# The output stage of an FFT filter with soft experts: combine weights on strips of 32 PE rows in float32r

## The chip, the cores and the metric

The kernel runs on one core of a Trainium2 chip. The time is what the device takes for one execution, in microseconds (us); work that the host does before and after is outside it. Before the change it is 431.18 us, the median of three runs (430.67, 431.18 and 431.85). Engines have these names: PE is TensorE (PEld its weight loads), DVE is VectorE, ACT is ScalarE, POOL is GpSimd, SP is the engine that here issues the DMA transfers.

## The reference

The input x is 8 batches of 2496 rows with 256 features. First it is filtered along the rows by a Fourier transform; then a layer of soft experts (8 experts with 4 slots each, so 32 slots) is applied to all 19968 filtered rows together:

```
X = rfft(x, axis=1);  y = irfft(X * F, n=2496)      # F: 1249 x 256, complex
logits = y @ phi                                    # 19968 x 32
d = softmax of logits over all rows                 # dispatch weights, one column per slot
slot_input = d.T @ y                                # 32 x 256
slot_out[e] = relu(slot_input[e] @ w1[e]) @ w2[e]   # hidden size 1024
c = softmax of logits over the 32 slots of a row    # combine weights
out = c @ slot_out                                  # 19968 x 256, float32
```

The last line is the output stage: for each row a product of its 32 combine weights with the 32 x 256 matrix slot_out. It writes 20.45 MB.

## The kernel before, in words

The transform of a batch is factored: 2496 = 39 x 64, with the row number written as 64 s1 + s2. The host lays out x so that a step i (0 to 21) holds up to three values of s2 (j = 0, 1, 2; PK = 3), each with its 39 values of s1, on 117 partitions (KR = 117). A table (RUNS) says which s2 belongs to a step and a j: in steps 0 to 15 j counts 0, 16 and 32 upwards, in steps 16 to 19 it counts 48, 52 and 56, and steps 20 and 21 hold the last four, s2 = 60 to 63 (step 20 three of them, step 21 one). The stages ahead of the output work through the batches in a pipeline, form the logits in the layout of these steps, and gather the slot inputs over groups of batches (GROUPS). For each group a tile with the exponentials of the logits is left (lgs; the first two groups are parked in DRAM and read back) with 117 partitions and, for every step, batch and slot, one element; r_all holds the reciprocals of the row sums. Then the expert products run (lines 786 to 820), in strips of 32 PE columns, with weights read from DRAM, and slot_out stands in PSUM, four times over on 128 partitions.

The output stage begins at line 821. It uses float32r, in which a matmul streams faster but keeps fewer bits, and makes up for the bits with high and low parts: so_h is slot_out rounded to float32r, and so holds so_h on partitions 0 to 63 and the remainder on 64 to 127. For the combine weights the same is done in `combine` (line 837), called for up to four steps at once, six times a batch:

- GpSimd multiplies the exponentials by the reciprocals (c1, line 848).
- ScalarE casts the product to float32r, and GpSimd subtracts this from the product (cr, lines 856 and 857). Each step then has 2 x 2 x 32 = 128 columns: high, low, high, low. These stand against the two halves of so, so that one matmul over 128 rows adds all four partial products.
- TensorE transposes each step by itself (line 860), 22 transposes a batch, to 128 partitions by 117 columns.
- VectorE casts the transposed tile into st (line 866), a tile with one column for each of the 2496 rows of the batch, and in the same pass puts the columns in an order in which rows that are neighbours in the output lie together (main for 2048 rows, rest for 448).

`blocks` (line 885) then multiplies: a matmul takes 128 (or, in rest, 112) columns of st as weights and so as the moving operand with 256 columns, two matmuls to a PSUM bank of 512 columns. ScalarE or VectorE copies the bank to a tile in SBUF, ob, which holds 8 output rows for each of 128 partitions, or obr (4 rows on 112 partitions). Six PSUM banks in three pools with two buffers each are taken in turn. When 8 rows (4 in the first and the last batch) of ob are full, SP issues a transfer to the output; so a batch has two transfers of ob with 1 MB each (four with 512 KB) and one of obr with 448 KB. There are four buffers of ob, two of obr, two of st.

Each engine works in the order of its own queue. The order in the queues is made when the kernel is built, by a planner that simulates the instructions with costs of its own and can place work of a later step ahead of work that must wait; buffers from the pools come free when their last reader is done.

Of the kernel before, what the change touches and what calls it, by code (L numbers as in the profile page):

```python
# [30 lines left out]
M1, MB, RP, RB = 32, 16, 112, 4  # L31
OC = 8
NE, SPE, FF = 8, 4, 1024
# [23 lines left out]
SB = 2  # L57
# [22 lines left out]
def shape_constants():  # L80
# [53 lines left out]
    def put(name, a):  # L134
        blocks.append((name, a))
# [27 lines left out]
    put("e0", e0)  # L163
    off, pos = {}, 0
# [25 lines left out]
def x_layout(x):  # L190

    s2 = np.array([[run_of(i, j) for i in range(NI)] for j in range(PK)])
    a = x.reshape(BATCH, N1, N2, DIM)[:, :, s2]
    return np.ascontiguousarray(a.transpose(0, 2, 1, 3, 4)).reshape(BATCH, KR, NI, DIM)


@with_exitstack
def fft_soft_moe(ctx, tc, x, fr, fi, fny, phi, w1, w2, cst, w1q, bmat, out):
# [623 lines left out]
    so = const.tile([P, DIM], F32R, name="so")  # L822
    nc.scalar.copy(so_h, po)
    nc.scalar.copy(so[0:64], po[0:64])
    nc.vector.tensor_tensor(out=so[64:128], in0=po[64:128], in1=so_h.bitcast(F32)[64:128], op=ALU.subtract)
# [4 lines left out]
    obp_cm, obp = open_pool("obp", 4, "right")  # L830
# [4 lines left out]
    steps_of = [(16, 4), (20, 2)] + [(i, 4) for i in range(0, MB, 4)]  # L835

    def combine(b, i0, n, st):
# [5 lines left out]
        c1 = tail.tile([KR, 4, SLOTS], F32, tag="c1", name=f"c1_{b}_{i0}")  # L843
        for h in range(2):
            lo, hi = max(i0, h * NH), min(i0 + n, (h + 1) * NH)
            if lo < hi:
                a = slice(lo - h * NH, hi - h * NH)
                nc.gpsimd.tensor_tensor(
                    out=c1[:, lo - i0 : hi - i0],
                    in0=cl[:, a, b2, h],  # L850
                    in1=rv[:, a, b2, h : h + 1].broadcast_to([KR, hi - lo, SLOTS]),
                    op=ALU.mult,
                )
        cr = tail.tile([KR, 4, 2, 2, SLOTS], F32R, tag="cr", name=f"cr_{b}_{i0}")
        cb = c1[:, 0:n].rearrange("s a (o e) -> s a o e", o=1).broadcast_to([KR, n, 2, SLOTS])
        nc.scalar.copy(cr[:, 0:n, :, 0], cb)  # L856
        nc.gpsimd.tensor_tensor(out=cr[:, 0:n, :, 1], in0=cb, in1=cr.bitcast(F32)[:, 0:n, :, 0], op=ALU.subtract)  # L857
        pt = ps_t.tile([P, 4, KR], F32, tag="t", name=f"ct_{b}_{i0}")
        for k in range(n):
            nc.tensor.transpose(pt[:, k, :], cr.bitcast(F32)[:, k].rearrange("s o q e -> s (o q e)"), ident[0:KR, 0:KR])  # L860
# [90 lines left out]
```

## Time and profile before

| What | Value |
|---|---|
| Median of three runs | 431.18 us |
| Profiled execution, its own time | 433.28 us |
| Its span, first to last instruction | 431.5 us |
| Mean granted TensorE clock | 0.974 of full speed |
| Busy: PE, PEld, DVE, ACT, POOL | 384.2, 291.9, 286.7, 236.1, 232.7 us |
| Moved by DMA | 107.00 MB, mean 248 GB/s |

The profile is one execution. A matmul's end is modelled and matmuls overlap, so a busy PE is not a PE at its peak. Idle time of an engine that does not hold up the rest costs nothing. Where the text speaks of a wait, the profile has inferred from semaphores who released whom. In rows by windows the busy times stand in the order PE, PEld, DVE, ACT, POOL, then the granted clock as a share of full speed, the DMA share and GB/s. In rows by shape the first number behind the bar is the busy time in us, the second the mean of one instruction in ns; SPq is SP's queue. The DMA share is the mean busy share of the 16 DMA engines in a stretch; a little over 1 can occur.

### The profile page before, as it was taken

Reading aid. Unit: us, or ns where it says so; the run is one execution under the profiler, and the core shown is the slowest. Engines: PE = TensorE matmul, PEld = TensorE weight load, DVE = VectorE, ACT = ScalarE, POOL = GpSimd, SP = SyncE. Lnnn points to the kernel's source line nnn. Section 1 sums busy time; section 2 is a strip of 40 time slices with the busy share of each in tenths; the row PEclk is TensorE's granted clock in tenths of the full one; section 3 lists DMA queues with packets and bytes.
Section 4 is the critical chain, followed back from the end, with each engine's and each line's share of the span. In section 5 each row is a group of like instructions: output and inputs, shape, how many; then the busy total and the mean of one; then the engine's idle time right before and its main releaser. Section 6 shows DMA issues by size and latency. Waiting matters only on the chain. (4 is left out here: it accounts for less than half of the span.)

```text
span 431.5 us, 12191 instructions
## 1 busy us (share of the span) xinstructions
PE 384.2 (89%) x4705; PEld 291.9 (68%) x4705; DVE 286.7 (66%) x571; ACT 236.1 (55%) x513; POOL 232.7 (54%) x290
## 2 busy tenths in 40 slices
PE   8677988999998999999989999989989798888882
PEld 3244866878877787887868688877867344677762
DVE  1342655876989955878996468994587223778882
ACT  2386566666577655856783343452464112767772
POOL 0047778797867565955965155652200003878870
PEclk9679999999999999999999999999999999989997
DMA  8999999999899687978995434322499992779887
GB/s 216 235 310 303 329 297 330 328 271 323 241 272 331 233 235 194 301 201 255 273 283 163 150 100 123 111 83 80 132 363 297 295 291 71 297 286 352 350 343 272
DMA packets 61818, 107.00 MB, mean 248 GB/s; under 512 B 6142, under 2 KB 37758, under 8 KB 60226
## 3 DMA queue, kind: packets, MB, share of 16 engines
q1 hardware_dynamic: 61762, 106.24, 77.8%
q8 instruction: 37, 0.61, 0.6%
q14 instruction: 19, 0.16, 0.1%
HBM read 63.48 MB, written 42.74 MB: 246 GB/s over the span
## 5 line engine op out<-in xcount | busy, mean ns | idle before, releaser
L273 POOL TENSOR_TENSOR xl<-xt,xh 117x512 fp32r<-117x512 f32 x77 | 102.9, 1350 | 54.4 <-ACT xh L272 52.9
L317 PE MATMUL x<-b_t,ash 128*128 128x128 f32 x640 | 90.2, 281 | 7.9 <-DMA ash<-a_dram 4.1
L317 PEld LDWEIGHTS x<-b_t,ash 128*128 128x128 f32 x640 | 79.7, 191 | 19.8 <-issue 6.1
L334 POOL TENSOR_TENSOR yt<-yt,t 128x256 f32<-128x256 f32 x80 | 65.9, 825 | 41.3 <-DVE t L331 29.6
L330 DVE TENSOR_TENSOR yt<-x,fr_t 128x512 f32<-128x512 f32 x80 | 54.7, 684 | 43.1 <-PE x L317 40.0
L272 ACT CAST xh<-xt 117x512 fp32r<-117x512 f32 x77 | 46.8, 622 | 38.8 <-DMA xt<-in_x 14.1
L346 ACT COPY y<-t 128x512 f32<-128x512 f32 x80 | 46.5, 591 | 34.3 <-PE t L344 28.6
L857 POOL TENSOR_TENSOR cr<-c,cr 117x256 fp32r<-117x256 f32 (+1 forms) x48 | 32.2, 689 | 53.1 <-ACT cr L856 52.6
L290 ACT COPY at<-s 120x512 f32<-120x512 f32 x83 | 48.4, 587 | 22.2 <-PE s L283 10.3
L331 DVE TENSOR_TENSOR t<-x,fi_t 128x512 f32<-128x512 f32 x80 | 54.3, 679 | 0.0
L344 PE MATMUL t<-cst_t,yt 128*128 128x128 f32 x320 | 48.6, 276 | 0.6 <-POOL yt L334 0.4
L333 DVE TENSOR_TENSOR yt<-yt,t 128x256 f32<-128x256 f32 x60 | 42.6, 719 | 0.8
L344 PEld LDWEIGHTS t<-cst_t,yt 128*128 128x128 f32 x320 | 37.2, 141 | 7.8 <-issue 3.2
L286 PE MATMUL s<-xh,w1h 117*120 117x512 f32 x77 | 36.2, 470 | 4.8 <-ACT xh L272 4.1
L890 PE MATMUL out<-so,st 128*128 128x256 f32 (+1 forms) x160 | 30.2, 325 | 6.6 <-DVE st L866 6.4
L866 DVE CAST st<-ct 128x384 fp32r<-128x384 f32 (+1 forms) x112 | 32.4, 361 | 5.4 <-PE ct L860 5.2
L333 POOL TENSOR_TENSOR yt<-yt,t 128x256 f32<-128x256 f32 x20 | 16.2, 812 | 30.8 <-DVE t L331 24.5
L286 PE MATMUL s<-xl,w1h 117*120 117x512 f32 x77 | 32.6, 423 | 0.3 <-POOL xl L273 0.2
L890 PEld LDWEIGHTS out<-so,st 128*128 128x128 f32 (+1 forms) x160 | 24.5, 216 | 12.2 <-DVE st L866 11.4
L286 PE MATMUL s<-xh,w1l 117*120 117x512 f32 x77 | 31.4, 408 | 0.0
L856 ACT CAST cr<-c 117x256 fp32r<-117x256 f32 (+1 forms) x48 | 17.5, 391 | 22.4 <-PE ct L860 13.4
L860 PE MATMUL ct<-cst_t,cr 117*128 117x117 f32 x176 | 25.1, 275 | 3.6 <-POOL cr L857 2.4
(111 smaller groups left out, 587.9 us busy)
## 6 DMA issues: line engine op xcount, KB each, us to landing
ash<-a_dram SPq DMA_DIRECT2D x80, 256.0 KB
a_dram<-at SPq DMA_DIRECT2D x80, 240.0 KB
xt<-in_x SPq DMA_DIRECT2D x40, 448.0 KB
w<-in_w SPq DMA_DIRECT2D x64, 256.0 KB
out<-ob SPq DMA_DIRECT2D x12, 1024.0 KB
out<-ob SPq DMA_DIRECT2D x8, 512.0 KB
out<-obr SPq DMA_DIRECT2D x8, 448.0 KB
xt<-in_x SPq DMA_DIRECT2D x8, 224.0 KB
```

The lines of the kernel that those rows point to most:

```text
L272: act.copy(xh, xs)
L273: pool_e.tensor_tensor(out=xl, in0=xs, in1=xh.bitcast(F32), op=ALU.subtract)
L286: pe.matmul(ps, w, xx, start=(n == 0), stop=(n == 2))
L290: act.copy(at, ps)
L317: pe.matmul(ps[:, 2 * k + dh].rearrange("q r c -> q (r c)"), ash[:, k, dh * P : (dh + 1) * P], b_t[:, t0 + k, :], start=True, stop=True,)
L330: dve.tensor_tensor(out=yt, in0=ps, in1=frv, op=ALU.mult)
L331: dve.tensor_tensor(out=t2, in0=ps[:, :, ::-1, :], in1=fiv, op=ALU.mult)
L333: add.tensor_tensor(out=yt[:, :, 1, :], in0=yt[:, :, 1, :], in1=t2[:, :, 1, :], op=ALU.add)
L334: pool_e.tensor_tensor(out=yt[:, :, 0, :], in0=yt[:, :, 0, :], in1=t2[:, :, 0, :], op=ALU.subtract)
L344: pe.transpose(pt[:, k, dh, :], yt[:, c % 2, 2 * k + dh].rearrange("q r c -> q (r c)"), ident)
L346: act.copy(y, pt.rearrange("k p h d -> k p (h d)"))
L890: nc.tensor.matmul(pr[0:rows, kk, :], lhs(k + kk), so, start=True, stop=True)
```

## The change

The steps of a batch are grouped in fives of four (QUADS). For one quad, the 4 x 32 combine weights of four steps stand side by side as 128 columns and go through one transpose, in float32, without high and low parts. After it, partitions 32 k to 32 k + 31 hold the 32 slots of the k-th step of the quad. The last four values of s2 (THIRDS) can't be grouped so: their weights are spread over 4 x 32 columns with a mask of ones and zeros (table third), and one matmul with a table of three stacked unit matrices (fold) does the transpose and picks out the 39 rows that are wanted.

Only then are the high and low parts made, by `split`: ScalarE casts PSUM to st[:, 0], and VectorE subtracts that from PSUM into st[:, 1]. The tile st now has 2 x 624 columns for a batch.

The output matmuls use 32 rows each: for strip k, the weights are 128 (or 112) columns of st on partitions 32 k to 32 k + 31, the moving operand is so_h or so_l on the same partitions, and four of them (high by high, high by low, low by high, low by low) add up in a PSUM bank. The four strips take turns, and each writes into a bank of its own. ScalarE empties the banks of strips 0 and 2, VectorE those of 1 and 3. The rows leave the device in the order in which the steps hold them; the host puts them in order afterwards (out_rows). The transfers keep their sizes. There are three buffers of st in place of two and six of ob in place of four.

```diff
-        cr = tail.tile([KR, 4, 2, 2, SLOTS], F32R, tag="cr", name=f"cr_{b}_{i0}")
-        nc.scalar.copy(cr[:, 0:n, :, 0], cb)
-        nc.gpsimd.tensor_tensor(out=cr[:, 0:n, :, 1], in0=cb, in1=cr.bitcast(F32)[:, 0:n, :, 0], op=ALU.subtract)
-        for k in range(n):
-            nc.tensor.transpose(pt[:, k, :], cr.bitcast(F32)[:, k].rearrange("s o q e -> s (o q e)"), ident[0:KR, 0:KR])
...
+    def split(st, lo, hi, src):
+
+        nc.scalar.copy(st[:, 0, lo:hi], src)
+        nc.vector.tensor_tensor(out=st[:, 1, lo:hi], in0=src, in1=st.bitcast(F32)[:, 0, lo:hi], op=ALU.subtract)
...
+        c1 = tail.tile([KR, 2, NH, SLOTS], F32, tag="c1", name=f"c1_{b}")
         for h in range(2):
+            rb = rv[:, :, b2, h : h + 1].broadcast_to([KR, NH, SLOTS])
+            nc.gpsimd.tensor_tensor(out=c1[:, h], in0=cl[:, :, b2, h], in1=rb, op=ALU.mult)
+        cq = tail.tile([KR, 2, 4, SLOTS], F32, tag="cr", name=f"cr_{b}")
+        nc.gpsimd.tensor_copy(cq[:, 0, 0:3], c1[:, 0, 8:11])
+        nc.gpsimd.tensor_copy(cq[:, 0, 3:4], c1[:, 1, 8:9])
+        for lo, hi, i in ((0, 3, 20), (3, 4, 21)):
+            mask = C("third", lo, hi).rearrange("s (k o) -> s k o", o=1).broadcast_to([KR, hi - lo, SLOTS])
+            src = c1[:, 1, i - NH : i - NH + 1].broadcast_to([KR, hi - lo, SLOTS])
+            nc.gpsimd.tensor_tensor(out=cq[:, 1, lo:hi], in0=src, in1=mask, op=ALU.mult)
+        pt = ps_t.tile([P, 4, KR], F32, tag="t", name=f"ct_{b}_0")
+        for n, quad in enumerate(QUADS[0:4]):
+            h, a = divmod(quad[0], NH)
+            nc.tensor.transpose(pt[:, n, :], c1[:, h, a : a + 4].rearrange("s a e -> s (a e)"), ident[0:KR, 0:KR])
+        split(st, 0, 4 * KR, pt.rearrange("q n s -> q (n s)"))
+        pt = ps_t.tile([P, KR + N1], F32, tag="t", name=f"ct_{b}_1")
+        nc.tensor.transpose(pt[:, 0:KR], cq[:, 0].rearrange("s a e -> s (a e)"), ident[0:KR, 0:KR])
+        nc.tensor.matmul(
+            pt[:, KR : KR + N1], cq[:, 1].rearrange("s a e -> s (a e)"), C("fold"), start=True, stop=True
+        )
+        split(st, 4 * KR, SQ, pt)
+
+    def blocks(st, m0, rows, ob, k0):
+
+        nm = 2 if rows == P else 1
+        prs = []
+        for k in range(4):
+            pool, tag = outs[(nout[0] + k) % 3]
+            prs.append(pool.tile([P, nm, DIM], F32, tag=tag, name=f"out_{nout[0]}_{k}"))
+        for mm in range(nm):
+            c0 = (m0 + mm) * P
+            for n in range(4):
+                for k in range(4):
+                    q = slice(32 * k, 32 * k + 32)
+                    nc.tensor.matmul(
+                        prs[k][0:rows, mm, :],
+                        st[q, n // 2, c0 : c0 + rows],
+                        (so_h, so_l)[n % 2][q, :],
+                        start=(n == 0),
+                        stop=(n == 3),
+                    )
+        for k in range(4):
+            copy = nc.scalar.copy if k % 2 == 0 else nc.vector.tensor_copy
+            copy(ob[0:rows, k0 + nm * k : k0 + nm * (k + 1), :], prs[k][0:rows])
+        nout[0] += 1
...
+        combine(b, st)
+        for i0 in range(0, MB, OC):
+            ob = obp.tile([P, OC, DIM], F32, tag="ob", name=f"ob_{b}_{i0}")
+            blocks(st, i0 // 4, P, ob, 0)
+            ends = (4, 8) if b in (OUT_ORDER[0], OUT_ORDER[-1]) else (8,)
+            for lo, hi in zip((0,) + ends, ends):
+                nc.sync.dma_start(om[:, i0 + lo : i0 + hi, :], ob[:, lo:hi, :])
         obr = obp.tile([P, RB, DIM], F32, tag="obr", name=f"obr_{b}", bufs=2)
+        blocks(st, 4, RP, obr, 0)
         nc.sync.dma_start(orest, obr[0:RP])
```

## Rows read from the trace of the kernel before

**Rows 1.** Windows, output stage: us, busy per engine (x instructions), clock, DMA share, GB/s.

```profile
372.00:380.00 8.00, 6.52 (x44) 5.24 (x44) 6.53 (x18) 5.29 (x12) 6.32 (x14) 1.00 0.77 296
380.00:388.00 8.00, 7.82 (x46) 6.72 (x44) 5.94 (x17) 5.63 (x13) 6.50 (x15) 0.79 0.68 256
...
396.00:404.00 8.00, 6.68 (x45) 5.50 (x46) 6.60 (x19) 5.48 (x12) 7.34 (x16) 1.00 0.95 373
...
412.00:420.00 8.00, 6.72 (x47) 5.55 (x46) 6.72 (x20) 5.98 (x15) 6.59 (x14) 1.00 0.90 356
420.00:428.00 8.00, 3.44 (x21) 2.82 (x20) 3.61 (x8) 2.95 (x6) 0.74 (x1) 0.89 1.01 367
```

**Rows 2.** The same view in stretches of 2 us.

```profile
366.00:368.00 2.00, 1.94 (x15) 1.53 (x15) 1.61 (x5) 1.97 (x5) 1.74 (x5) 1.00 0.17 68
...
374.00:376.00 2.00, 1.77 (x13) 1.34 (x14) 1.91 (x5) 1.64 (x4) 1.74 (x5) 1.00 0.15 57
...
428.00:430.00 2.00, 0.00 (x0) 0.00 (x0) 0.00 (x0) 0.00 (x0) 0.00 (x0) 0.50 0.29 104
```

**Rows 3.** Timeline of SP's queue, output transfers: start us, us, issues merged.

```profile
366.82 3.48 SPq L913 DMA_DIRECT2D out<-ob  x4
370.72 0.34 SPq L918 DMA_DIRECT2D out<-obr  x1
...
378.79 0.33 SPq L918 DMA_DIRECT2D out<-obr  x1
...
387.88 1.69 SPq L918 DMA_DIRECT2D out<-obr  x1
...
424.94 0.48 SPq L918 DMA_DIRECT2D out<-obr  x1
```

**Rows 4.** Waits of SP's queue, 340 to 431.5: total us, times, longest.

```profile
SPq L913 <- DVE ob L894: 45.9, 18, 11.1
```

**Rows 5.** Waits of the compute engines, 362 to 431: total us, times, longest.

```profile
PEld out L890 <- DVE st L866: 11.4, 24, 1.3
...
PEld ct L860 <- POOL cr L857: 6.4, 12, 1.5
```

**Rows 6.** Lines by shape, 330 to 431.5: busy us, mean ns | idle before.

```profile
L890 PE MATMUL out<-so,st 128*128 128x256 f32 x128 | 23.6, 315 | 6.6 <-DVE st L866 6.4
L892 ACT COPY ob<-out 128x512 f32<-128x512 f32 x42 | 23.1, 589 | 9.1 <-PE out L890 8.7
...
L894 DVE COPY ob<-out 128x512 f32<-128x512 f32 x22 | 15.1, 685 | 5.9 <-issue 2.3 <-ACT ob L892 1.7 <-ACT cr L856 1.0
L811 PE MATMUL o<-w,ht 128*32 128x256 f32 x128 | 10.4, 383 | 0.3
...
L794 PE MATMUL h<-w,sit 128*32 128x512 f32 x64 | 7.5, 597 | 0.3 <-DVE sit L784 0.3
L890 PEld LDWEIGHTS out<-so,st 128*112 128x112 f32 x32 | 7.2, 297 | 0.0
L848 POOL TENSOR_TENSOR c<-cl,r_all 117x128 f32<-117x128 f32 x16 | 6.4, 411 | 0.0
...
L811 PEld LDWEIGHTS o<-w,ht 128*32 128x32 f32 x128 | 4.5, 109 | 5.4 <-DMA w<-in_w 2.5 <-issue 0.7
...
L848 POOL TENSOR_TENSOR c<-cl,r_all 117x32 f32<-117x32 f32 x4 | 1.0, 243 | 0.0
...
L819 DVE COPY osb<-o 128x256 f32<-128x256 f32 x2 | 0.8, 424 | 8.2 <-PE o L811 8.2
...
L823 ACT CAST so_h<-slot_out 128x256 fp32r<-128x256 f32 x1 | 0.4, 365 | 0.0
```

**Rows 7.** Timeline of TensorE, three stretches: start us, us, instructions merged.

```profile
350.26 1.93 PE L811 MATMUL o<-w,ht 128*32 128x256 f32 x32
...
365.32 1.33 PE L890 MATMUL out<-so,st 128*128 128x256 f32 x8
...
416.75 0.76 PE L860 MATMUL ct<-cst_t,cr 117*128 117x117 f32 x6
```

More of the change, by code (lines that the diff above doesn't have):

```diff
@@ L56 @@
 WL = 5
-SB = 2
+SB = 3
 STEPS = "IB P FC TC TC TC C XC C XC CC AA X - - - ATATAT"
@@ L163, in shape_constants @@
     put("e0", e0)
+    third = np.zeros((PK, N1, 4))
+    for k, (_, j) in enumerate(THIRDS):
+        third[j, :, k] = 1.0
+    put("third", third.reshape(KR, 4))
+    put("fold", np.tile(np.eye(N1), (PK, 1)))
     off, pos = {}, 0
@@ L194, in x_layout, with out_rows @@
     return np.ascontiguousarray(a.transpose(0, 2, 1, 3, 4)).reshape(BATCH, KR, NI, DIM)
+def out_rows():
+    row = np.zeros(SEQ, np.int64)
+    for k in range(4):
+        cols = [(q[k], j, s1) for q in QUADS for j in range(PK) for s1 in range(N1)]
+        cols += [THIRDS[k] + (s1,) for s1 in range(N1)]
+        for c, (i, j, s1) in enumerate(cols):
+            m, p = divmod(c, P)
+            r = p * MB + m // 2 * 8 + 2 * k + m % 2 if m < 4 else MB * P + p * RB + k
+            row[N2 * s1 + run_of(i, j)] = r
+    return row
 @with_exitstack
@@ L821, in fft_soft_moe @@
     so_h = const.tile([P, DIM], F32R, name="so_h")
[L822 removed]
+    so_l = const.tile([P, DIM], F32R, name="so_l")
     nc.scalar.copy(so_h, po)
[L824 to L825 removed]
+    nc.vector.tensor_tensor(out=so_l, in0=po, in1=so_h.bitcast(F32), op=ALU.subtract)
     late_cm.__exit__(None, None, None)
@@ L885, in blocks @@
-    def blocks(lhs, rows, ob, k):
-        pool, tag = outs[nout[0] % 3]
-        pr = pool.tile([P, 2, DIM], F32, tag=tag, name=f"out_{nout[0]}")
-        for kk in range(2):
-            nc.tensor.matmul(pr[0:rows, kk, :], lhs(k + kk), so, start=True, stop=True)
-        if nout[0] % 3 != 1:
-            nc.scalar.copy(ob[0:rows, k : k + 2, :], pr[0:rows])
-        else:
-            nc.vector.tensor_copy(ob[0:rows, k : k + 2, :], pr[0:rows])
+            rb = rv[:, :, b2, h : h + 1].broadcast_to([KR, NH, SLOTS])
@@ L905, in fft_soft_moe @@
[L905 to L913 removed]
+        om = out[t0 : t0 + MB * P].rearrange("(p i) d -> p i d", i=MB)
@@ L916, in fft_soft_moe @@
-        for k in range(0, RB, 2):
-            blocks(lambda i: rest[:, :, i], RP, obr, k)
+        blocks(st, 4, RP, obr, 0)
         nc.sync.dma_start(orest, obr[0:RP])
```

65 lines of the change are left out of this document (11 added, 54 removed).

## The prediction

> **What bounds the kernel now.** I read the busy time by stretches first, then SP's queue and what it waits for, then the waits of the compute engines, then the costs by line and shape. The stage that the diff touches begins at the last matmuls of the expert products (about 362 us) and lasts to the end of the span at 431.5 us. In the three 8 us stretches inside it that ran at the full clock no engine is full: TensorE is busy 6.5 to 6.7 of 8, VectorE 6.5 to 6.7, GpSimd 6.3 to 7.3, ScalarE 5.3 to 6.0, and the DMA share is 0.77 to 0.95 [rows 1]. Only the last stretch, 420 to 428, has the DMA at 1.01. So neither the bytes nor one engine sets the pace. In the 2 us stretches the DMA falls to a share of 0.15 and 57 GB/s at 374 to 376 [rows 2]: there nothing is ready to be sent. SP's queue says the same: it waits 45.9 us in total for the last copy into an output buffer [rows 4], and the bound is how fast a batch of output is computed.
>
> SP's issues give the period [rows 3]: the last transfer of the first batch (tile obr) is issued at 370.72 and that of the eighth at 424.94, seven periods in 54.22 us, 7.75 us each. Within it the engines wait for each other: TensorE's weight loads for VectorE's casts into st, 11.4 us, and for GpSimd's low parts, 6.4 us [rows 5]. Each four steps go GpSimd, ScalarE, GpSimd, TensorE, VectorE, TensorE, and a copy out.
>
> The last bytes: 68 GB/s in 366 to 368 is 0.14 MB and 104 GB/s in 428 to 430 is 0.21 MB [rows 2], so at some 400 GB/s the transfers run from about 367.6 to 428.6 us: 61 us for 20.45 MB (19968 rows of 1 KB). Then 2.9 us pass to the end of the span.
>
> **The change part by part, for one batch.**
>
> *GpSimd.* Removed: the low parts and the products in 128-element pieces; GpSimd was busy 6.3 to 7.3 us of 8, some 6.5 us a batch of 7.75 [rows 1]. Added: two products of 117x352. A 117x128 product takes 411 ns and a 117x32 one 243 [rows 6], which is 1.75 ns an element, so 411 + 224 x 1.75 = 803 ns each. Two copies and two masked products of 96 and 32 elements lie on the same line, 355 and 243 ns. Sum 2 x 0.80 + 2 x 0.60 = 2.8 us. No row shows a copy on GpSimd at this size; nothing speaks for it to be above a product, and if it were twice that, 3.4 us would still be under the period.
>
> *ScalarE.* Removed: the casts to cr. Added: casts of 128x468 and 128x156 out of PSUM. Between 589 ns for 512 elements and 365 for 256 [rows 6] they come to 0.55 and 0.28. Its copies out: four of 128x512 and two of 112x256: 4 x 0.589 + 2 x 0.365 = 3.09. Sum 3.9 us, before about 5.4 (5.3 to 6.0 of 8) [rows 1].
>
> *VectorE.* Removed: all casts into st, in which rows were put in order. Added: two subtractions, which by 685 ns for 512 and 424 for 256 elements [rows 6] come to 0.64 and 0.32; copies out 4 x 0.685 + 2 x 0.424 = 3.59. Sum 4.55, before about 6.4 [rows 1].
>
> *TensorE, transposes.* 22 become 5 and one folding matmul. Six in a row took 0.76 us [rows 7], about 0.1 each: 2.2 us become 0.6.
>
> *TensorE, output matmuls.* 20 of 128 rows become 80 of 32 rows, in rounds of four, one for each strip. This is the one price that the trace doesn't show. Today eight in a row with their loads take 1.33 us [rows 7]; less one length of 0.315 [rows 6] over seven, that is 0.15 us for a load and a matmul. From below: four strips side by side cost what one whole matmul costs, 0.15 us for a round of four. From above: one after the other, 0.60. The nearest row is the second product of the experts, which uses four strips of 32 columns: 32 float32 matmuls of 256 moving columns in 1.93 us [rows 7], so with 0.383 [rows 6] for the last, 0.05 us each and 0.20 a round. One such matmul alone streams (597 - 383) / 256 = 0.84 ns a column [rows 6], 0.21 us for 256 columns: the four column strips stream wholly beside each other, and their loads cost nothing. I take the same for row strips, 0.15 us a round; 20 rounds make 3.0 us. (The Trainium skill, TensorE: Matmul & The Clock Gate, "Measured speedup vs the span model", has four row strips 3.07 times as fast as one after the other, not four times. By that a round would be 0.60 / 3.07 = 0.195 us, the period below 6.65 and the span 423.8; no row here shows row strips, and the column strips come nearer to four times.)
>
> The blocks that read st in steps of four elements also go: their weight loads take 297 ns [rows 6]. They are contiguous after; this is in the 0.15.
>
> *A wait that the change adds.* A group of matmuls now fills four of the six output banks at once, tiles 4j to 4j+3, and tile t needs tile t-6 emptied. So the third and fourth strip of a group wait for the first and second copy of the group before. TensorE is in order, so all rounds behind it wait, and the copies out and SP behind those. Price: the matmul's 0.315, VectorE's copy 0.685 and about 0.05 of signals, less the 0.04 of a normal step: 1.0 us after a large group, and 0.315 + 0.424 = 0.75 after the small one: 2.75 a batch. The next batch's transposes and splits lie in these gaps (0.6 us of TensorE). If they don't, they cost at most their 0.6 us.
>
> *The sum.* TensorE's loop is 20 x 0.15 + 2.75 = 5.75 us a batch. All other engines are lower. What is late next is the DMA: where it was busy it moved 373 / 0.95 = 393 GB/s in 396 to 404, 356 / 0.90 = 395 in 412 to 420, and 367 / 1.01 = 363 in 420 to 428 [rows 1]; 2.556 MB a batch is 6.5 us at 393 and 7.0 at 363. So the period goes from 7.75 to 6.5, set by the DMA. More buffers (six of ob, three of st) let compute run ahead, so it stays full.
>
> *Ends.* The first issue was at 366.82 [rows 3]. Before it, the low part of the expert output is one subtraction as now, and ScalarE has one cast of 0.365 fewer [rows 6]. With four strips the first transfer waits for a full group of 32 matmuls, some 1.2 us, where eight did before; the transposes may be done earlier, since st is small. I count this as nothing, within 1 us either way. The 22 KB of new constants are loaded long before this stage, among transfers of 256 KB and more: nothing. The host's reordering lies outside the device time.
>
> Span: 431.5 - 7 x (7.75 - 6.5) = 422.75. Checked by bytes: 20.45 MB at 390 GB/s is 52.4 us from 367.6, and 2.9 behind it: 422.9. The profiled execution took 433.28 us, 1.78 more than its span, so this gives 424.6; the median shown, 431.18, is 2.1 below that execution, so on its scale the time is 422.5. I put it at 422.8.
>
> **The rivals.**
>
> *The row strips don't run beside each other.* Then each of the 80 loads and matmuls costs what 20 cost now. For it: no row has 32-row operands at partition 32 or above, and each strip loads 128 columns of weights, where the column strips load only 32, in 109 ns [rows 6]. Against: the independence of column strips. Fully one after the other, a round is 0.60, the period 20 x 0.60 + 2.75 = 14.75, the span 431.5 + 7 x 7.0 = 480.5. Loads alone queued: a round of about 0.4 gives 10.75 and 452.5. It decides from a round of (7.75 - 2.75) / 20 = 0.25 us: above that the change loses. (The Trainium skill, same page, "LDWEIGHTS (loading the stationary operand)", says that a load of 32 rows takes as long as one of 128. That alone would put four loads where one stood; no run here shows whether four strips share them.)
>
> *The granted clock falls.* In 380 to 388 it was 0.79 [rows 1] and the period from 378.79 to 387.88 was 9.09 us [rows 3]. Matmul bursts with gaps of 1 us and fewer transposes may bring this more often. At the lower level, 1.2 GHz, a round is 0.30, and each of the three gaps is longer by another 0.315 of its matmul: 6.0 + 3.7 = 9.7. Two batches of eight: 422.75 + 2 x 3.2 = 429; all: 445. Against: TensorE stays about as often active as now, and waiting for the DMA costs nothing.
>
> *The gain goes into the split.* The subtraction stands in VectorE's queue ahead of the copies out and waits for ScalarE's cast, which waits for TensorE's transposes. If no gap holds this, 0.55 + 0.64 + 0.6 add to 5.75: 7.5 a batch, and the time is 428 to 432, no change. For it: VectorE and ScalarE have only 1 us free after each large group.
>
> **How the numbers follow.** A change within 0.3% (1.3 us) can't be told from none. The forecast, at 417.5 to 428 (DMA at 425 GB/s to a round of 0.22 us), has 0.66. Strips one after another: 0.16, at 445 to 485. The clock: 0.09, at 426 to 445. The split: 0.09, at 427 to 433. Faster: 0.66 and about 0.04 of the last two, 0.70. Same: 0.06. Slower: 0.24. The range 417 to 436 leaves out the strips in series and the long clock falls, about 0.2.
>
> **What would show it.** Right: 80 output matmuls a batch, four of which start within some 0.15 us of each other; six transposes a batch; obr issues 6.5 us apart; a DMA share of 0.95 or more from 372 us on, with SP or the copies waiting for transfers; GpSimd at 2.8 us a batch, VectorE 4.6, ScalarE 3.9. Wrong: rounds above 0.25 us with TensorE without idle time; a clock of 0.5 over many stretches; or a DMA share that stays at 0.8, with TensorE waiting for ScalarE's and VectorE's copies longer than 1 us a group.

## The result, and the profile after

The changed kernel takes 426.91 us (median of 20 runs, 424.05 to 432.09), the kernel before 431.23 us (median of 20 runs, 429.49 to 433.88). The ratio is 0.9915, with a 95% interval of 0.9894 to 0.9935: 2.8 to 4.6 us less. The medians are of all executions; the ratios of this document leave out executions more than 1.5% above the fastest of their kernel. The direction was forecast and the time lies in the range, but the gain is half of what was forecast or a little less: 4.3 us by the medians and 3.7 by the ratio, instead of 8.4.

The profiled execution took 425.78 us, its span 423.9. The two profiled executions are 7.5 us apart and so show more than the medians do: before's lies at the upper end of its runs, after's 1.1 us below its median. The cast so_h, with which the output stage begins, starts at 359.4 us after and at 363.3 before, in work that the change does not touch; so 3.9 of the 7.6 us between the spans lie ahead of the stage. For this reason stages are compared from this cast on; the rows themselves count from the start of the span.

Windows of the kernel after, against [rows 1] and [rows 2] (columns as there):

```profile
364.00:372.00 8.00, 8.00 (x153) 7.12 (x153) 6.39 (x14) 4.95 (x13) 4.70 (x12) 1.00 1.02 383
...
380.00:388.00 8.00, 8.00 (x147) 7.14 (x144) 6.54 (x14) 5.64 (x15) 0.00 (x0) 1.00 1.01 394
...
396.00:404.00 8.00, 6.81 (x76) 6.19 (x71) 3.33 (x6) 2.80 (x6) 0.00 (x0) 0.50 1.01 369
404.00:412.00 8.00, 2.98 (x28) 2.34 (x25) 2.10 (x4) 1.72 (x4) 0.00 (x0) 0.50 1.00 370
...
416.00:417.00 1.00, 0.00 (x0) 0.00 (x0) 0.00 (x0) 0.00 (x0) 0.00 (x0) 0.50 0.82 274
417.00:418.00 1.00, 0.00 (x0) 0.00 (x0) 0.00 (x0) 0.00 (x0) 0.00 (x0) 0.50 0.45 172
...
422.00:423.00 1.00, 0.00 (x0) 0.00 (x0) 0.00 (x0) 0.00 (x0) 0.00 (x0) 0.50 0.03 12
```

The gaps in the DMA are gone: its share is 1.00 or more from 364 to 412 us, where it was 0.68 to 0.95 in the stretches from 372 to 420 [rows 1]. GpSimd is done before 380 us, the copies by 412. Then comes what the forecast did not have: the share falls from 0.82 in 416 to 417 to 0.03 in 422 to 423. For six microseconds some of the 16 DMA engines still write while the others are done.

SP's queue of the kernel after, against [rows 3]:

```profile
363.05 2.91 SPq L926 DMA_DIRECT2D out<-ob  x4
366.28 0.94 SPq L929 DMA_DIRECT2D out<-obr  x1
...
386.55 0.96 SPq L929 DMA_DIRECT2D out<-obr  x1
...
393.59 0.33 SPq L929 DMA_DIRECT2D out<-obr  x1
...
409.09 1.74 SPq L929 DMA_DIRECT2D out<-obr  x1
```

While buffers last, the obr issues are (386.55 - 366.28) / 4 = 5.07 us apart; later, 7 us and more. Waits of the compute engines, 362 to 424 us, against [rows 5]:

```profile
ACT obr L912 <- DMA out<-obr: 7.5, 4, 2.9
...
DVE obr L912 <- DMA out<-obr: 6.7, 4, 2.6
PEld out L903 <- ACT obr L912: 3.0, 3, 1.6
```

The copies wait for transfers, and TensorE for these copies; its waits for casts and low parts [rows 5] are gone. The chain that ended last (start, us, what) says the same:

```profile
381.24 11.41 DMA out<-obr
...
393.59 14.16 DMA out<-obr
```

Lines by shape of the kernel after, against [rows 6]:

```profile
L912 DVE COPY ob<-out 128x512 f32<-128x512 f32 x32 | 20.6, 684 | 7.6 <-PE out L903 7.3
L912 ACT COPY ob<-out 128x512 f32<-128x512 f32 x32 | 17.4, 592 | 13.4 <-PE out L903 11.4 <-POOL cr L878 1.3 <-ACT st L859 0.6
...
L871 POOL TENSOR_TENSOR c<-cl,r_all 117x352 f32<-117x352 f32 x8 | 6.2, 801 | 24.7 <-PE ct L885 22.7 <-PE ct L882 2.0
...
L912 DVE COPY obr<-out 112x256 f32<-112x256 f32 x16 | 6.1, 417 | 6.7 <-DMA out<-obr 6.7
...
L912 ACT COPY obr<-out 112x256 f32<-112x256 f32 x16 | 5.2, 379 | 7.5 <-DMA out<-obr 7.5
L860 DVE TENSOR_TENSOR st<-ct,st 128x468 fp32r<-128x468 f32 x8 | 5.1, 644 | 2.7 <-ACT st L859 2.4
L859 ACT CAST st<-ct 128x468 fp32r<-128x468 f32 x8 | 4.5, 567 | 10.6 <-PE ct L882 10.6
...
L878 POOL TENSOR_TENSOR cr<-c,cst_t 117x96 f32<-117x96 f32 x8 | 2.8, 349 | 0.0
...
L859 ACT CAST st<-ct 128x156 fp32r<-128x156 f32 x8 | 2.5, 313 | 0.0
L860 DVE TENSOR_TENSOR st<-ct,st 128x156 fp32r<-128x156 f32 x8 | 2.5, 310 | 0.0
...
L873 POOL COPY cr<-c 117x96 f32<-117x96 f32 x8 | 2.1, 263 | 2.2 <-PE ct L886 2.2
```

TensorE's timeline of the kernel after, against [rows 7]:

```profile
361.43 0.29 PE L903 MATMUL out<-so_l,st 32*128 32x256 f32 x4
361.54 0.29 PE L903 MATMUL out<-so_h,st 32*128 32x256 f32 x4
361.66 0.29 PE L903 MATMUL out<-so_l,st 32*128 32x256 f32 x4
361.78 0.29 PE L903 MATMUL out<-so_h,st 32*128 32x256 f32 x4
...
362.14 0.38 PE L903 MATMUL out<-so_h,st 32*128 32x256 f32 x2
362.26 0.38 PE L903 MATMUL out<-so_l,st 32*128 32x256 f32 x2
```

Four matmuls of 32 rows begin together every 0.115 us: the strips run beside each other. From 362.02 on the rounds have two strips only, and these too begin 0.12 us apart.

### The profile page after: what moved, and what is told of

The parts are those of the page before. It is cut to its first block, busy times and chain, and to the rows that moved or that the text cites. A ratio compares the mean times of both kernels' runs of the same rounds, so it can differ in the third digit from the quotient of the medians.

```text
span 423.9 us, 12672 instructions
## 1 busy us (share of the span) xinstructions
PE 374.5 (88%) x5065; PEld 291.3 (69%) x5065; DVE 269.8 (64%) x496; ACT 218.6 (52%) x475; POOL 201.9 (48%) x234
## 4 chain that ended last, share of the span: by engine, by line
PE 61%; DMA 16%; DVE 12%; ACT 3%; issue 2%; SPq 2%; POOL 0%; ACTq 0%; DVEq 0%
PE x L339 15%; PE s L308 8%; PE t L366 6%; DMA out<-obr 6%; DMA xt<-in_x 6%; PE s L581 4%; PE l L377 4%; PE out L903 3%; PE v L423 3%; PE dt L537 2%; DMA ash<-a_dram 2%; DVE t L353 2%; PE o L833 2%; PE lg L450 2%; PE s L305 2%
## 5 line engine op out<-in xcount | busy, mean ns | idle before, releaser
L295 POOL TENSOR_TENSOR xl<-xt,xh 117x512 fp32r<-117x512 f32 x77 | 103.0, 1350 | 52.7 <-ACT xh L294 49.9
L339 PE MATMUL x<-b_t,ash 128*128 128x128 f32 x640 | 91.5, 284 | 6.1 <-DMA ash<-a_dram 3.1
L339 PEld LDWEIGHTS x<-b_t,ash 128*128 128x128 f32 x640 | 81.2, 194 | 17.0 <-issue 5.0
L903 PE MATMUL out<-so_h,st 32*128 32x256 f32 (+1 forms) x320 | 36.3, 329 | 3.3 <-ACT obr L912 2.4
L903 PE MATMUL out<-so_l,st 32*128 32x256 f32 (+1 forms) x320 | 34.4, 311 | 0.0
L903 PEld LDWEIGHTS out<-so_h,st 32*128 32x128 f32 (+1 forms) x320 | 29.9, 206 | 6.5 <-ACT obr L912 3.0
L903 PEld LDWEIGHTS out<-so_l,st 32*128 32x128 f32 (+1 forms) x320 | 30.3, 209 | 0.0
L377 PE MATMUL l<-yt,phi_t 128*32 128x128 f32 x640 | 26.1, 278 | 0.9 <-ACT y L368 0.7
L912 DVE COPY ob<-out 128x512 f32<-128x512 f32 x32 | 20.6, 684 | 7.6 <-PE out L903 7.3
```

What stands on the lines that cost most here:

```text
L295: pool_e.tensor_tensor(out=xl, in0=xs, in1=xh.bitcast(F32), op=ALU.subtract)
L339: pe.matmul(ps[:, 2 * k + dh].rearrange("q r c -> q (r c)"), ash[:, k, dh * P : (dh + 1) * P], b_t[:, t0 + k, :], start=True, stop=True,)
L903: nc.tensor.matmul(prs[k][0:rows, mm, :], st[q, n // 2, c0 : c0 + rows], (so_h, so_l)[n % 2][q, :], start=(n == 0), stop=(n == 3),)
```

## The experiments

The theory from these rows: the computation is as quick as forecast and the DMA is now the bound, but the price of the transfers was too low. Rivals: the computation holds the transfers up (buffers of obr, the granted clock at 0.50, 1.2 of 2.4 GHz, from about 394 us on, the first transfer); or transfers and computation disturb each other. The table is read from the traces: the start of the cast so_h, the first and the last packet of the output transfers, the end of the span (us), and the stage, which is the span's end less so_h. A packet's record does not name its DMA engine. But there are 448 packets of 4 bytes for the 28 transfers, 16 for each, and where the text says when the engines end, it takes the last 16 of them.

| Trace | so_h | first | last | between | end | stage |
|---|---|---|---|---|---|---|
| before | 363.3 | 367.7 | 429.8 | 62.1 | 431.5 | 68.2 |
| before_again | 361.9 | 366.3 | 428.2 | 61.9 | 429.9 | 68.0 |
| before_buf | 360.2 | 364.6 | 426.7 | 62.2 | 428.5 | 68.3 |
| after | 359.4 | 363.9 | 422.3 | 58.4 | 423.9 | 64.5 |
| after_again | 360.8 | 365.2 | 425.9 | 60.6 | 427.4 | 66.6 |
| after_third | 360.5 | 365.0 | 423.3 | 58.3 | 424.9 | 64.4 |
| obr4 | 362.3 | 366.8 | 424.9 | 58.1 | 426.5 | 64.2 |
| undo_buf | 356.2 | 360.7 | 419.3 | 58.6 | 420.7 | 64.5 |
| three | 359.4 | 364.1 | 421.4 | 57.3 | 422.8 | 63.4 |
| dma_only | 360.6 | 362.8 | 419.1 | 56.3 | 420.4 | 59.8 |
| dma_only2 | 360.6 | 362.9 | 419.4 | 56.5 | 420.8 | 60.2 |

**The same kernels again.** before_again, after_again and after_third change nothing.

> The kernel before, unchanged, for a second trace. Its first profiled execution lasted 433.28 us against a median of 431.2, and the kernel after was profiled 1.1 us under its own median, so the two traces lie 7.5 us apart and the medians 4.3. If part of the 3.9 us by which slot_out is ready earlier in the trace after (so_h cast at 359.4 instead of 363.3) is chance, this trace has that cast nearer to 361 and the last matmuls of the experts' second product without the 2.6 us wait for weights. If it comes from the change, the cast is at 363 again. Time ratio 1.000.

> The kernel after, unchanged, for a second trace. Theory DMA: the stage ends when the slowest of the 16 DMA engines has written its share; the DMA share is about 1.0 from the first output transfer to some 52 us later, then falls over several us to zero as one engine after another ends, and first traffic to last traffic is about 58 us again. Theory buffers: the tail is a matter of when the last obr is issued (409.1); then the tail follows that issue and not the DMA share. Median about 4 us under before.

> The kernel after once more, on the same chip, for the comparison: 425 to 428 us, a tail of 5 us or more at the end.

Measured against the kernel before on the same chip: before_again 1.0015 (0.9983 to 1.0047), after_again 0.9895 (0.9853 to 0.9938), after_third 0.9904 (0.9871 to 0.9938). so_h moves by 7 us among the eleven traces of the table, also between traces of one kernel, so a difference of two spans says little here and the stage says more. It is 68.2 on the mean of the first three rows and 64.8 of the five with after's matmuls and transfers: 3.4 of the 4.3 us of the medians lie in the stage, and the rest is within that scatter ahead of it. Whether the tail follows the last issue (theory buffers in after_again) is not decided by these traces: that issue came 53.8 us behind so_h in after_again, 49.7 in after and 50.4 in after_third, and the stage of after_again is the longest, but a late issue can also come of slow transfers.

**Transfers alone, computation alone.** dma_only keeps every transfer as it is and computes nothing in the stage; compute_only computes everything and issues the transfers of the last batch alone.

```diff
 dma_only
+    ob = obp.tile([P, OC, DIM], F32, tag="ob", name="ob_all")
+    nc.vector.memset(ob, 0.0)
...
-        combine(b, st)
-            blocks(st, i0 // 4, P, ob, 0)
-        blocks(st, 4, RP, obr, 0)
 compute_only
-            for lo, hi in zip((0,) + ends, ends):
+            for lo, hi in zip((0,) + ends, ends) if b == OUT_ORDER[-1] else ():
...
-        nc.sync.dma_start(orest, obr[0:RP])
+        if b == OUT_ORDER[-1]:
+            nc.sync.dma_start(orest, obr[0:RP])
```

> The output stage without its computation: the combine weights, transposes, splits, output matmuls and copies are left out, and the same 28 transfers are issued one after the other from two tiles filled once. It measures the transfers by themselves. Theory DMA: first traffic to last traffic is 52 to 58 us, so the time is at most 4 us under the kernel after; if the late engines come from the computation's use of SBUF, the spread at the end is gone and it is nearer to 52. Theory buffers or compute: well below, 50 us or less for the transfers, and 6 us or more under the kernel after.

> The kernel after without the output transfers of the first seven batches (their rows are not written); all computation stays. It shows how fast the changed computation goes when nothing waits for a transfer. Theory DMA: the loop runs at 20 rounds x 0.115 us + 2.75 us of waits for banks, 5.0 us a batch, so the last copies come near 402 us and the time is some 15 to 20 us under the kernel after. Theory compute: a period of 6.5 us or more, and the time falls by less than 8 us.

dma_only takes 422.12 us (0.9807, 0.9775 to 0.9839), compute_only 408.86 (0.9465, 0.9411 to 0.9519). In compute_only the copies into obr, two a batch on ScalarE (shortest/median/longest ns, first and last start), run

```profile
L912 ACT COPY obr<-out x16: 372/380/388, 365.9 to 400.2; 112x256 f32<-112x256 f32 x16
```

from 365.9 to 400.2 us, about 4.9 us a batch. So the computation is not what fills 6.5 us and more, and the transfers alone already take the 422.8 us that were forecast for the whole. Windows of dma_only:

```profile
396.00:404.00 8.00, 0.00 (x0) 0.00 (x0) 0.00 (x0) 0.00 (x0) 0.00 (x0) 0.50 1.01 394
404.00:412.00 8.00, 0.00 (x0) 0.00 (x0) 0.00 (x0) 0.00 (x0) 0.00 (x0) 0.50 1.01 380
...
413.00:414.00 1.00, 0.00 (x0) 0.00 (x0) 0.00 (x0) 0.00 (x0) 0.00 (x0) 0.50 0.98 340
414.00:415.00 1.00, 0.00 (x0) 0.00 (x0) 0.00 (x0) 0.00 (x0) 0.00 (x0) 0.50 0.55 188
...
418.00:419.00 1.00, 0.00 (x0) 0.00 (x0) 0.00 (x0) 0.00 (x0) 0.00 (x0) 0.50 0.06 20
```

With nothing beside them they show the same ending: the share drops from 414 on, the last engine writes until 419.1. The packets' time, shared evenly over 16 engines, is 52.7 us; the engine that ends last takes 56.3.

**Is it the computation after all?** obr4 gives obr four buffers, undo_buf takes the buffers of st and ob back to two and four, three leaves the product low by low out and takes the products with so_h first, and before_buf gives the kernel before six buffers of ob.

```diff
 obr4
-        obr = obp.tile([P, RB, DIM], F32, tag="obr", name=f"obr_{b}", bufs=2)
+        obr = obp.tile([P, RB, DIM], F32, tag="obr", name=f"obr_{b}", bufs=4)
 undo_buf (the second pair of lines the other way round in before_buf)
-SB = 3
+SB = 2
...
-    obp_cm, obp = open_pool("obp", 6, "right")
+    obp_cm, obp = open_pool("obp", 4, "right")
 three
-            for n in range(4):
+            for n in range(3):
...
-                        st[q, n // 2, c0 : c0 + rows],
-                        (so_h, so_l)[n % 2][q, :],
+                        st[q, n % 2, c0 : c0 + rows],
+                        (so_h, so_l)[n // 2][q, :],
...
-                        stop=(n == 3),
+                        stop=(n == 2),
```

> Four buffers of obr in place of two. In the trace after, the copies out wait 14.2 us for obr buffers still being sent, and TensorE falls to the low clock behind them. Theory buffers: without these waits the last issue comes 5 us or more earlier and the time falls by 3 us or more. Theory DMA: the last issue comes earlier, the transfers queue up instead, and the time stays within 1 us of the kernel after.

> The kernel after with the buffers of before: two of st, four of ob. Theory DMA: computation needs 5 us a batch and the transfers 6.6, so fewer buffers still keep the queue full; within 1 us of the kernel after. Rival: the gain came from the added buffers; then the time goes back by 2 us or more towards 431.

> The kernel after with three products in place of four (the product of the two low parts is left out), so 60 output matmuls a batch, and with both products against so_h first, so the first matmuls wait less for so_l. Theory DMA: only the first transfer counts; it comes 0.3 to 0.8 us earlier after the so_h cast, the time falls by that or less. Theory compute: a quarter fewer matmuls, 0.6 us a batch, 4 us in all.

> The kernel before with six buffers of ob in place of four. Theory compute (before is bound by its computation, 7.75 us a batch): the time stays within 1 us of before. Rival: the added buffers alone bring the gain: 2 us or more faster.

obr4: 428.12 us, 0.9932 (0.9904 to 0.9961), not faster than after_again on the same chip (425.46). Windows of obr4:

```profile
388.00:396.00 8.00, 7.99 (x150) 7.29 (x153) 6.34 (x13) 5.28 (x13) 0.00 (x0) 1.00 1.01 393
...
404.00:412.00 8.00, 0.15 (x2) 0.00 (x0) 0.42 (x1) 0.37 (x1) 0.00 (x0) 0.50 1.00 372
```

TensorE keeps its full clock to 396 us and all computation is over by some 405, four microseconds earlier than in the kernel after and seven earlier behind so_h, and yet the stage is 64.2 us against 64.5. The last issue, which both theories had earlier, came 49.0 us behind so_h (49.7 in after). So the chain through obr and the clock of 0.50 from 394 us on were where the waiting showed, not what caused it. undo_buf: 426.85 (0.9839, 0.9788 to 0.989), stage 64.5 as with the added buffers; before_buf: 430.15 (0.9988, 0.9956 to 1.002). The buffers are worth nothing measurable by themselves in either kernel. three: 427.14 (0.9891, 0.9856 to 0.9927), a quarter of the output matmuls fewer and no clear gain; it was also to issue its first transfer earlier, and this was a miss: 3.9 us behind so_h, 3.6 in the kernel after.

**Do they disturb each other?** decoupled computes everything and sends all transfers from one tile that is filled once, so that neither waits for the other.

```diff
+    ob_all = obp.tile([P, OC, DIM], F32, tag="oball", name="ob_all", bufs=1)
...
-                nc.sync.dma_start(om[:, i0 + lo : i0 + hi, :], ob[:, lo:hi, :])
+                nc.sync.dma_start(om[:, i0 + lo : i0 + hi, :], ob_all[:, lo:hi, :])
...
-        nc.sync.dma_start(orest, obr[0:RP])
+        nc.sync.dma_start(orest, ob_all[0:RP, 0:RB, :])
```

> All computation of the kernel after, and all 28 transfers, but the transfers are read from one tile filled beforehand and wait for no copy (what is written is not the result). The transfers alone took 56.3 us from first to last packet, in the kernel after 58.1 to 60.7. Theory contention (computation beside the transfers makes single packets slower and the engines more uneven): 58 us or more here too, time 1.5 us or more above the transfers alone. Theory coupling (the transfers start and pause with the copies): 56 to 57 us, time within 1 us of the transfers alone, 422.1.

428.0 us (0.9872, 0.982 to 0.9924). The time is inconclusive: in its trace TensorE had a clock of 0.50 to 0.55 from 364 us on, busy 8.0 of 8 us, and computed until 427 us, some 8 us a batch, which is not the case that was to be looked at. Its transfers, which waited for no copy, took 60.2 us, where theory contention had 58 or more and theory coupling 56 to 57. This speaks for contention, in one trace.

**What makes the transfers slow?** All of these leave the computation out of the stage and change only the transfers. dma_halves sends each ob in two halves of 64 partitions, dma_two issues obr from ScalarE's queue, dma_noobr does not send obr, and dma_pairs sends the same bytes as 39 rows on all 128 partitions for each pair of batches, in transfers of 8, 4 and 3 rows. dma_only2 is dma_only again; after_halves does the computation, with the halves.

```diff
 dma_halves, after_halves
-                nc.sync.dma_start(om[:, i0 + lo : i0 + hi, :], ob[:, lo:hi, :])
+                for p in (0, 64):
+                    nc.sync.dma_start(om[p : p + 64, i0 + lo : i0 + hi, :], ob[p : p + 64, lo:hi, :])
 dma_two
-        nc.sync.dma_start(orest, obr[0:RP])
+        nc.scalar.dma_start(orest, obr[0:RP])
 dma_pairs
+    for pair in range(4):
+        t0 = OUT_ORDER[2 * pair] * SEQ
+        om = out[t0 : t0 + 2 * SEQ].rearrange("(p i) d -> p i d", p=P)
+        cuts = [0, 8, 16, 20, 28, 36, 39]
...
+        for lo, hi in zip(cuts, cuts[1:]):
+            src = ob if hi - lo != 3 else obr
+            nc.sync.dma_start(om[:, lo:hi, :], src[:, 0 : hi - lo, :])
```

> The output stage without its computation, as in the run of the transfers alone, but each transfer of ob is issued as two, for partitions 0 to 63 and 64 to 127, so that each DMA engine gets rows of other partitions and addresses. Theory address (some partitions or addresses are slow, and the engine that has them ends last): the work is mixed, the spread at the end shrinks, 53 to 55 us from first to last packet, time 1.5 us or more under 422.1. Theory engine (an engine is slow, or packets are slow by chance): still about 56 us, time within 1 us.

> The transfers alone again, with those of obr issued by ScalarE's queue instead of SP's, so that two queues feed the engines. Theory: the engines are full, so which queue feeds them doesn't matter: 56 us, time within 1 us of 422.1. Rival: one queue in order leaves early engines idle; two let them go on, 1.5 us or more faster.

> The kernel after with each ob transfer in two, by halves of the partitions, computation unchanged. Theory address: 1.5 us or more under the kernel after. Theory engine: within 1 us of it.

> The transfers alone (no computation of the output stage; what is written is not the result), all 20.45 MB in the same sizes of packet, but every transfer reads 128 partitions: two batches are cut into 128 partitions of 39 rows, so no transfer of 112 partitions is left. Theory partitions: the transfers of obr, where each engine reads seven partitions instead of its eight, make engines meet on the same part of SBUF, slow packets there and leave engines behind; without them the first to last packet falls from 56.3 us to 50 to 53 and the engines end within 2 us of each other. Theory chance: packets are slow whatever they read; 55 us or more.

> The transfers alone without those of obr: 16.78 MB, 18% fewer bytes. By the rate at which ob transfers go, 415 GB/s, the obr transfers are worth 3.67 / 0.415 = 8.8 us; if they also hold up others, more. Theory partitions: 11 us or more less than the transfers alone. Theory chance: 9 to 10 us less.

> The transfers alone once more, for the comparison on this chip and for a second trace: 56 us from first to last packet, one to three engines several us behind the others.

| Run | us | ratio to before |
|---|---|---|
| dma_halves | 441.20 | 1.0212 (1.0140 to 1.0284) |
| after_halves | 442.73 | 1.0271 (1.0222 to 1.0321) |
| dma_two | 423.72 | 0.9834 (0.9777 to 0.9891) |
| dma_only2 | 422.28 | 0.9782 (0.9710 to 0.9854) |
| dma_pairs | 416.55 | 0.9655 (0.9575 to 0.9736) |
| dma_noobr | 408.08 | 0.9451 (0.9392 to 0.9510) |

Windows of dma_pairs:

```profile
396.00:404.00 8.00, 0.00 (x0) 0.00 (x0) 0.00 (x0) 0.00 (x0) 0.00 (x0) 0.50 1.01 417
...
411.00:412.00 1.00, 0.00 (x0) 0.00 (x0) 0.00 (x0) 0.00 (x0) 0.00 (x0) 0.50 1.00 392
412.00:413.00 1.00, 0.00 (x0) 0.00 (x0) 0.00 (x0) 0.00 (x0) 0.00 (x0) 0.50 0.47 181
413.00:414.00 1.00, 0.00 (x0) 0.00 (x0) 0.00 (x0) 0.00 (x0) 0.00 (x0) 0.50 0.00 0
```

At the same share of 1.01 it moves 403 to 419 GB/s where dma_only moves 380 to 403, and the share falls from 1.00 to nothing within 2 us: the first packet is written at 362.9, the engines end between 412.4 and 412.6, so the transfers take 49.7 us (the expectation of pairs below has 50.2). Windows of dma_noobr:

```profile
388.00:396.00 8.00, 0.00 (x0) 0.00 (x0) 0.00 (x0) 0.00 (x0) 0.00 (x0) 0.50 1.00 417
...
403.00:404.00 1.00, 0.00 (x0) 0.00 (x0) 0.00 (x0) 0.00 (x0) 0.00 (x0) 0.50 0.64 254
404.00:405.00 1.00, 0.00 (x0) 0.00 (x0) 0.00 (x0) 0.00 (x0) 0.00 (x0) 0.50 0.00 0
```

Without obr the end is as sharp. 3.67 MB at 417 GB/s would be 8.8 us; leaving them out saves 14.2. So the transfers of 112 partitions cost 5.4 us more than their bytes: on the mean packets take longer (393 instead of 417 GB/s makes 3 us on 20.45 MB; of 3456 packets with data 162 last over 350 ns in dma_only, none in dma_pairs and dma_noobr), and the engines are done at different times. Short rows are not the reason, since dma_pairs has transfers of 4 and 3 rows too, on 128 partitions. One rival was not separated: the rows of an obr transfer make one block in the output, and in dma_pairs the rows of neighbouring partitions lie 39 KB apart; so the addresses changed with the partitions. Windows of dma_halves:

```profile
396.00:404.00 8.00, 0.00 (x0) 0.00 (x0) 0.00 (x0) 0.00 (x0) 0.00 (x0) 0.50 0.96 278
```

Both theories of dma_halves were missed: it is 19 us slower. Nearly full engines and 278 GB/s: which partitions a transfer reads bears on what a busy engine moves. (The Trainium skill, SBUF — State Buffer, "Door 1: The DMA port swizzle (why [64,N] ≈ [32,N])", has 64 neighbouring partitions reach only one port of each of eight pairs. The trace agrees in direction: the page gives some 218 GB/s for 64 partitions, and this run, with the halves sent one behind the other and obr among them, moved 255 to 301.) after_halves shows that the computation beside them changes little in this: 1.5 us more than dma_halves. dma_two brings the engines' ends closer together, 419.1 to 421.4, but moves only 307 to 358 GB/s while both queues are at work (364 to 396 us), and gains nothing (423.72 against 422.28 us).

**A version of it.** pairs is the whole kernel with dma_pairs' transfers: st for two batches, 2 x 624 columns, of which nine blocks of 128 fill 36 rows a partition; the last 96 columns of each strip fill the other three, in pieces of 32 columns and in plain float32. pairs2 does this remainder in float32r, with 96 columns at once, and copies strip 3 in three pieces. In both the host's order of rows is changed to suit, obp has five buffers and st two.

```diff
 pairs
+            for mm in range(nm):
+                c0 = 9 * P + 32 * (lo + mm)
+                issue_rounds([product(pr[32 * k : 32 * k + 32, mm, :], k, st, c0, 32) for k in range(4)])
...
 pairs2
+        issue_rounds([product(prs[k][0:96, 0, :], k, st, 9 * P, 96) for k in range(4)])
...
+        for j, copy in enumerate((nc.vector.tensor_copy, nc.scalar.copy, nc.vector.tensor_copy)):
+            copy(ob[96:128, k0 + j, :], prs[3][32 * j : 32 * j + 32, 0, :])
```

> The kernel after with every output transfer on 128 partitions: the batches of the output stage go in pairs, a pair has 128 partitions of 39 rows, and the last 96 columns of each strip are multiplied in pieces of 32 columns (in float32, each strip into its own quarter of the partitions) so that they fill 128 partitions. Computation is otherwise that of the kernel after. Theory partitions: the transfers alone fell from 56.3 to 50.2 us and 422.2 to 416.6 us by this; with the computation beside them the kernel after should fall by 4 to 6 us, to 420 to 423, and the 16 DMA engines should end together, with no tail of several us. Theory contention (the computation, not the transfers' shape, makes the tail in the full kernel): less than 2 us.

> As the run of pairs, but the last 96 columns of each strip are multiplied in float32r like the rest, all four strips side by side, and come to 128 partitions by the copies out (strips 0 to 2 fill partitions 0 to 95 of a slot each, strip 3 is copied in three pieces to partitions 96 to 127). In pairs the float32 pieces held TensorE for 5.5 us at the end of each pair and the DMA share fell to 0.7 and 0.4. Theory partitions: now the DMA stays full, all 16 engines end together and the stage from the so_h cast to the end takes 55 to 58 us in place of 64 to 67; the time is 418 to 422. Theory contention: the transfers stay slow beside the computation, stage 62 us or more, time 425 or more.

pairs: 427.68 us, 0.992 (0.9886 to 0.9954), no better than the change itself. SP's queue in it:

```profile
369.69 0.90 SPq L955 DMA_DIRECT2D out<-obr  x1
375.18 0.33 SPq L957 DMA_DIRECT2D out<-obr  x1
```

Between the transfer of four rows and that of the last three lie 5.5 us: the float32 remainder leaves the DMA without work (a share of 0.80 in the window from 372 to 380 us, 0.42 from 404 to 412). In pairs2 this is 3.2 us or less. Its six executions took 419.2, 420.2, 427.1, 428.0, 428.2 and 428.8 us, in two groups, and no ratio is given for it. Windows of pairs2, of the execution of 419.2 us:

```profile
388.00:396.00 8.00, 7.39 (x118) 6.33 (x118) 6.20 (x13) 5.51 (x14) 2.39 (x6) 1.00 1.02 416
...
414.00:415.00 1.00, 0.00 (x0) 0.00 (x0) 0.00 (x0) 0.00 (x0) 0.00 (x0) 0.50 0.39 157
415.00:416.00 1.00, 0.00 (x0) 0.00 (x0) 0.00 (x0) 0.00 (x0) 0.00 (x0) 0.50 0.11 43
```

So with 128 partitions the full computation does reach 388 to 416 GB/s, engines that end between 413.8 and 416.1, and a stage of 58.1 us instead of 64.5. Its transfers take 51.9 us from the first packet to the last (364.2 to 416.1), those of after 58.4. The packets, their MB and the share of the 16 engines' time that they took, in after from 363.8 to 422.4, in pairs2 from 364.0 to 416.2 and in dma_pairs from 362.8 to 412.8:

```profile
q1 hardware_dynamic: 3904, 20.45, 93.2%
q1 hardware_dynamic: 3600, 20.45, 96.2%
q1 hardware_dynamic: 4032, 20.45, 100.7%
```

This is 54.6 us for an engine in after, 50.2 in pairs2 and 50.4 in dma_pairs. So with 128 partitions throughout, the computation beside the transfers does not make their packets longer. What the four longer executions spend is not seen, for they have no trace; the mean granted clock was 0.97 in the two short and 0.93 to 0.94 in the four long ones. That TensorE then holds up the transfers, at some 8 us a batch as in decoupled, is argued, not shown. No version is shown to beat the change reliably.

## Why the prediction was right in direction and wrong in size

*What bounded the kernel before.* Right: with the computation shortened, the DMA's gaps close, and compute_only shows that the stage's computation by itself now takes 4.9 us a batch, where the period was 7.75.

*The engines.* Right. From the lines by shape, GpSimd has 2 x 0.80 + 0.26 + 0.21 + 0.35 + 0.24 = 2.7 us a batch (forecast 2.8; the two 32-element pieces are 0.21 and 0.24), ScalarE 0.57 + 0.31 + 4 x 0.59 + 2 x 0.38 = 4.0 (3.9), VectorE 0.64 + 0.31 + 4 x 0.68 + 2 x 0.42 = 4.5 (4.55).

*TensorE.* Right that the strips run beside each other, wrong in both terms of its 5.75 us; the period was 5.07 where no buffer was missing. A round of four strips is 0.115 us, not 0.15, below the lower bound given. With it the sum would be 20 x 0.115 + 2.75 = 5.05 us, but that this agrees is luck. The wait of 2.75 us a batch for banks did not come as forecast: in compute_only TensorE is busy 7.7 to 8.0 of 8 us from 364 to 396, and its weight loads wait 1.9 us in all for copies between 362 and 400. What comes instead are rounds of two strips, 0.12 us apart like those of four (the timeline of TensorE above), so that a batch has more than 20 rounds. No run shows the 2.75. The loads of 32 rows last as long as those of 128 (183 and 189 ns, the medians of after and before), and do not add up: those of four strips fit into the same 0.115 us. The estimate of 0.195 us a round is not borne out. It rests on the ratio in TensorE: Matmul & The Clock Gate (the Trainium skill, "Measured speedup vs the span model"), which is for 512 columns; the ratio itself is not measured here, since no run has the strips one after another.

*What is late next: the DMA.* This is the step that failed, in the price and not in the name: "2.556 MB a batch is 6.5 us at 393 and 7.0 at 363. So the period goes from 7.75 to 6.5", and in the check "20.45 MB at 390 GB/s is 52.4 us from 367.6, and 2.9 behind it". That is 55.3 us from the first packet to the end of the span. Measured: 57.6 with the transfers alone, 60.0 in after and after_third, 62.2 in after_again. The rate itself was right: dma_only moved 380 to 403 GB/s while its engines were busy. The first 2.3 us of the miss are shown: 52.4 is the mean over 16 engines (52.7 measured in dma_only), but the stage ends with the slowest of them, 56.3 us behind the first packet, and the transfers of 112 partitions make them unequal; with 128 partitions throughout it is 49.7. The profile before had two hints. The share of 1.01 with 367 GB/s in its last window [rows 1], a full engine that moves less, was read as the bad end of a range and not as a property of the transfers. And the last 0.21 MB [rows 2] were put at 400 GB/s, so that the transfers seemed to end at 428.6 us; they ended at 429.8, and 1.2 of the 2.9 us behind them were the same uneven end:

```profile
429.00:430.00 1.00, 0.00 (x0) 0.00 (x0) 0.00 (x0) 0.00 (x0) 0.00 (x0) 0.50 0.07 29
```

The other 2.4 to 4.6 us appear only with computation beside the transfers. Their packets then take longer (54.4 to 55.4 us on the mean of the engines in the three traces of the kernel after, 52.7 and 53.1 alone). That transfers are issued as buffers fill, and not all at once, is not needed for it: in decoupled they waited for no copy and took 54.8, though in one trace at the half clock. Computation alone does not do it either: where all transfers have 128 partitions, the packets took the same time with it (pairs2) and without (dma_pairs), and pairs2's transfers lasted 51.9 us from first to last, where the forecast had 52.4. In that one trace the whole miss is gone with the transfers of 112 partitions. Why computation makes these dearer is not settled.

*Ends.* Right at the start: the first transfer is issued 3.6 us behind so_h after, 3.5 before.

*From the profiled execution to the median.* 2.1 us were taken off for before's execution lying above its median. so_h came 1.4 to 3.1 us earlier in the other traces of before, so this was right; it only cannot be read off one trace.

*The rivals.* Strips one after another: refuted by the rounds of 0.115 us. The clock: it did fall to 0.50 from about 394 us, behind waits of TensorE for transfers, and obr4, at the full clock to 396, ended no earlier. In decoupled it fell at the start of the stage, with TensorE busy; whether it counts in after's longer executions is open. The split: refuted by 4.9 us a batch in compute_only. None of the rivals was what happened; the missing one was a DMA whose slowest engine ends later than the mean.

## What to carry to other kernels

When the next bound will be the DMA, don't price it by bytes over the mean rate of busy stretches: send the same transfers alone, and look at when the engines end, not only at their mean share. Keep output transfers on all 128 partitions if the stage is to end with them; a share of 1.0 says that the engines are busy, not that they move what they could. And compare stages from an anchor inside the program, as two spans can differ by several microseconds ahead of the change.

## What the runs showed of the hardware that was not expected

- Four strips of 32 rows, 128 weight columns and 256 float32r columns each take 0.115 us together, loads included; two strips take 0.12.
- Transfers of 112 partitions among those of 128 cost 14.2 us (dma_only2 less dma_noobr) for bytes that at 417 GB/s would take 8.8; the engines then end 4.6 us apart instead of 0.2.
- With 128 partitions throughout, packets took the same time beside the computation (50.2 us an engine, pairs2) as alone (50.4, dma_pairs); with transfers of 112 among them 54.6 beside it (after) and 52.9 alone (dma_only).
- Transfers of 64 partitions, one half behind the other and obr among them, move 255 to 301 GB/s at a share of 0.85 to 1.01; all 128 partitions move 403 to 419.
- Two issuing queues, ob on one and obr on the other, moved 307 to 358 GB/s together while both were busy, and one alone 418 to 423 in the same run.
